# Loading the output weight in 4 KB rows and regrouping the attention outputs with selection matmuls, in a decode-attention kernel

## Chip, cores, metric

One core of one Trainium2 chip. The metric is the device time of one execution in microseconds (us). The span quoted with a profile runs from the first to the last instruction and is mostly about 1.8 us shorter than the time (the changed kernel: 194.7 of 196.47).

## The reference, cut to what matters

```python
B, Sq, D = 32, 1, 512                  # 32 sequences, one new token each
Hq, Hkv, Sk, Dh = 32, 8, 2048, 128
W = 512                                # only the last 512 cached tokens are attended
q = (x @ wq)                           # wq: [512, 4096], bf16
k, v = k_cache[:, :, Sk - W:], v_cache[:, :, Sk - W:]
o = softmax(q k^T * Dh**-0.5) v        # per batch and head
out = o.reshape(B, Sq, Hq * Dh) @ wo   # wo: [4096, 512] bf16, 4 MB
```

All tensors are bf16. The caches' windows are 33.5 MB each, wq and wo 4.2 MB each, so 75.5 MB must come from HBM. The profile of before confirms it: "HBM read 75.53 MB".

## The kernel before, the parts that matter

The core streams K and V of 32 batches through one DMA queue, issued by SyncE (SP). K and V loads are 512 KB each, in rows of 4 KB, one row per partition. TensorE (PE) transposes K, computes scores, transposes the probabilities and multiplies with V (PV). The attention output of a batch, already transposed (`d` on the partitions, 32 heads in the columns), is copied to `oT_sb`. The 4 MB of `wo` are loaded last on the same queue, into the place that `wq` has left, and are contracted with `oT_sb`, head by head.

```python
            sp.wait_ge(pe_qt, 1)
            for c in range(4):                                  # heads 0-9, 10-19, 20-27, 28-31
                h0, h1 = WO_CUT[c], WO_CUT[c + 1]
                sp.dma_start(
                    wo_sb[:, h0:h1, :],
                    wo[h0 * DH:h1 * DH, :].rearrange("(h d) n -> d h n", d=P),   # rows of 1 KB
                ).then_inc(sem_wo[c], 16)
            sp.wait_ge(dve_out, 1)
            sp.dma_start(
                out.rearrange("b s (c n) -> c (b s) n", c=4), out_sb[:, :]       # rows of 256 B
            ).then_inc(sem_out, 16)
# ...
            pe.wait_ge(dve_oT, B)
            for hq in range(HQ):
                if hq in WO_CUT:
                    pe.wait_ge(sem_wo[WO_CUT.index(hq)], 16)
                for c in range(4):                              # four column tiles of PE
                    ins = pe.matmul(
                        KT_ps[:, 0, :].bitcast(F32)[32 * c:32 * (c + 1), 0:128],
                        lhsT=oT_sb[:, :, hq],
                        rhs=wo_sb[:, hq, c * 128:(c + 1) * 128],
                        start=(hq == 0), stop=(hq == HQ - 1), tile_position=(0, 32 * c),
                    )
            ins.then_inc(pe_fin, 1)
# ... VectorE (DVE):
            dve.wait_ge(pe_fin, 1)
            dve.tensor_copy(out_sb[:, :], KT_ps[:, 0, :].bitcast(F32)[:, 0:128]).then_inc(dve_out, 1)
```

Partition `d` must hold row `128 * h + d` of `wo`, because that is where the attention output has its `d`. Consecutive rows of `wo` therefore lie on different partitions, and one contiguous piece is one row of 512 elements: 1 KB.

## Time and profile before

| | before |
|---|---|
| median of 3 runs | 198.06 us (197.87 to 198.22) |
| span of the profiled run | 196.5 us |
| PE / DVE / ACT busy | 73% / 51% / 29% |
| chain that ended last | SP's queue 52%, DMA 37%, PE 7% |

The kernel is bound by its loads. The row of the page that gives the GB/s moved in each of 40 equal slices (4.9 us each) shows it. Only the last four slices fall off.

```profile
GB/s 205 425 417 409 411 405 409 411 409 405 409 409 405 408 407 409 410 407 410 404 409 408 409 409 404 410 406 409 406 408 408 408 409 403 409 404 350 338 253 16
```

The view by windows of the end follows. Its columns are the window, its length, the busy us of each engine with the number of instructions, the granted share of PE's clock, the share of time in which the 16 DMA engines were busy, and the GB/s moved.

```profile
core 0: us, PE busy (x) PEld busy (x) DVE busy (x) ACT busy (x) POOL busy (x), PEclk, DMA share, GB/s
176.00:180.00 4.00, 2.22 (x66) 1.86 (x64) 0.38 (x2) 1.36 (x2) 0.00 (x0) 0.50 1.04 368
180.00:184.00 4.00, 2.02 (x64) 1.87 (x64) 0.38 (x2) 0.00 (x0) 0.00 (x0) 0.50 1.03 343
184.00:189.00 5.00, 1.38 (x44) 1.15 (x48) 0.00 (x0) 0.00 (x0) 0.00 (x0) 0.50 1.04 334
189.00:193.00 4.00, 2.33 (x76) 1.83 (x79) 0.00 (x0) 0.00 (x0) 0.00 (x0) 0.50 0.37 124
```

While `wo` is loaded the DMA engines are as busy as ever (share above 1.0), but move 334 to 368 GB/s instead of 408. After 189 us their share is 0.37 on average. PE's clock stands at half (0.50).

The timeline of the last instructions (start, duration, engine, line, operation, output and inputs, count, and in brackets how long the engine had been idle and what released it):

```profile
191.62 1.08 PE L301 MATMUL KT_ps<-w_sb,oT_sb 128*32 128x128 bf16 x32 [1.41 <-DMA w_sb<-in_wo_dram]
192.95 0.65 PE L301 MATMUL KT_ps<-w_sb,oT_sb 128*32 128x128 bf16 x16 [0.25 <-DMA w_sb<-in_wo_dram]
193.66 0.29 DVE L368 CAST out_sb<-KT_ps 128x128 bf16<-128x128 f32 x1 [10.70 <-PE KT_ps L301]
193.97 0.69 SPq L153 DMA_DIRECT2D out_dram<-out_sb  x1
```

So the end is a chain: the last `wo` load lands at about 192.9, 16 matmuls, one eviction, one store, and the span ends at 196.5.

### The profile page before, as it was taken

Reading aid. Unit: us, or ns where it says so; the run is one execution under the profiler, and the core shown is the slowest. Engines: PE = TensorE matmul, PEld = TensorE weight load, DVE = VectorE, ACT = ScalarE, POOL = GpSimd, SP = SyncE. Lnnn points to the kernel's source line nnn. Section 1 sums busy time; section 2 is a strip of 40 time slices with the busy share of each in tenths; the row PEclk is TensorE's granted clock in tenths of the full one; section 3 lists DMA queues with packets and bytes.
Section 4 is the critical chain, followed back from the end, with each engine's and each line's share of the span. In section 5 each row is a group of like instructions: output and inputs, shape, how many; then the busy total and the mean of one; then the engine's idle time right before and its main releaser. Section 6 shows DMA issues by size and latency. Waiting matters only on the chain.

```text
span 196.5 us, 6073 instructions
## 1 busy us (share of the span) xinstructions
PE 142.8 (73%) x2692; PEld 116.4 (59%) x2692; DVE 99.8 (51%) x187; ACT 56.5 (29%) x67; POOL 12.1 (6%) x43
## 2 busy tenths in 40 slices
PE   0448994987787797749786979779997599746423
PEld 0337773875575576637665858656975477535322
DVE  0006789645774479424952695457645647541000
ACT  3002434433262145203342325232432052320000
POOL 8102000000000010000000000000000000000000
PEclk9999999699999799985999797996699759955555
DMA  5999999999999999999999999999999999999970
GB/s 205 425 417 409 411 405 409 411 409 405 409 409 405 408 407 409 410 407 410 404 409 408 409 409 404 410 406 409 406 408 408 408 409 403 409 404 350 338 253 16
DMA packets 23374, 75.95 MB, mean 386 GB/s; under 512 B 2325, under 2 KB 6453, under 8 KB 22837
## 3 DMA queue, kind: packets, MB, share of 16 engines
q1 hardware_dynamic: 23300, 75.54, 97.5%
q8 instruction: 21, 0.34, 0.7%
q10 hardware_dynamic: 48, 0.03, 0.2%
q14 instruction: 5, 0.03, 0.0%
HBM read 75.53 MB, written 0.03 MB: 384 GB/s over the span
## 4 chain that ended last, share of the span: by engine, by line
SPq 52%; DMA 37%; PE 7%; issue 2%; DVE 0%
DMA K_sb<-in_k_cache_dram 32%; SPq L136 25%; SPq L128 18%; SPq L148 8%; DMA w_sb<-in_wo_dram 5%; PE KT_ps L229 4%; PE QO_ps L279 1%; PE S_ps L246 1%; SPq L122 1%; PE KT_ps L301 0%; SPq L110 0%; DVE out_sb L368 0%
## 5 line engine op out<-in xcount | busy, mean ns | idle before, releaser
L229 PE MATMUL KT_ps<-perm,K_sb 128*128 128x128 bf16 x1024 | 76.0, 238 | 20.7 <-DMA K_sb<-in_k_cache_dram 20.5
L324 DVE COPY KT_sb<-KT_ps 128x1024 bf16<-128x1024 bf16 x96 | 63.3, 687 | 54.0 <-PE KT_ps L229 53.7
L229 PEld LDWEIGHTS KT_ps<-perm,K_sb 128*128 128x128 bf16 x1024 | 67.5, 108 | 27.1 <-DMA K_sb<-in_k_cache_dram 26.0
L383 ACT ACTIVATE KT_sb<-KT_ps 128x1024 bf16<-128x1024 bf16 x32 | 32.7, 1023 | 81.8 <-PE KT_ps L229 81.8
L279 PEld LDWEIGHTS QO_ps<-PT_sb,V_sb 128*128 128x128 bf16 x1024 | 28.2, 98 | 17.4 <-issue 12.7
L279 PE MATMUL QO_ps<-PT_sb,V_sb 128*128 128x16 bf16 x1024 | 31.1, 171 | 3.7 <-DMA V_sb<-in_v_cache_dram 1.9
L346 DVE TENSOR_SCALAR P_ex<-P_f,recip 32x512 bf16<-32x512 f32 x32 | 25.3, 792 | 1.1
L246 PE MATMUL S_ps<-KT_sb,QBD 128*32 128x512 bf16 x256 | 21.4, 414 | 0.0
L401 ACT ACTIVATE PT_sb<-PT_ps 128x1024 bf16<-128x1024 bf16 x16 | 15.5, 1020 | 20.4 <-PE PT_ps L261 20.4
L261 PE MATMUL PT_ps<-ident,P_ex 128*128 128x128 bf16 x128 | 11.8, 266 | 9.6 <-DVE P_ex L346 9.6
L261 PEld LDWEIGHTS PT_ps<-ident,P_ex 128*128 128x128 bf16 x128 | 10.1, 122 | 10.7 <-DVE P_ex L346 10.7
L189 POOL COPY QBD<-QT_sb 128x32 bf16<-128x32 bf16 x32 | 7.4, 245 | 117.9 <-PE S_ps L246 108.0
L353 DVE CAST oT_sb<-QO_ps 128x32 bf16<-128x32 f32 x32 | 5.9, 183 | 8.9 <-PE QO_ps L279 8.8
L301 PE MATMUL KT_ps<-w_sb,oT_sb 128*32 128x128 bf16 x128 | 4.3, 313 | 6.6 <-DMA w_sb<-in_wo_dram 6.6
L207 PE MATMUL PT_ps<-xT_sb,w_sb 128*128 128x32 bf16 x128 | 4.1, 188 | 6.2 <-DMA w_sb<-in_wq_dram 6.2
L301 PEld LDWEIGHTS KT_ps<-w_sb,oT_sb 128*32 128x32 bf16 x128 | 3.3, 158 | 7.4 <-DMA w_sb<-in_wo_dram 4.7
L207 PEld LDWEIGHTS PT_ps<-xT_sb,w_sb 128*128 128x128 bf16 x128 | 3.7, 104 | 6.6 <-DMA w_sb<-in_wq_dram 4.6
L330 DVE TENSOR_REDUCE maxv<-S_ps 128x1 f32<-128x512 f32 x8 | 5.5, 691 | 4.0 <-PE S_ps L246 4.0
L391 ACT ACTIVATE P_f<-S_ps,negmax 128x512 f32<-128x512 f32 x8 | 5.5, 687 | 5.4 <-DVE negmax L332 5.4
L246 PEld LDWEIGHTS S_ps<-KT_sb,QBD 128*32 128x32 bf16 x256 | 3.9, 96 | 3.7 <-issue 1.0
L316 DVE CAST QT_sb<-PT_ps 128x512 bf16<-128x512 f32 x1 | 0.7, 691 | 10.0 <-PE PT_ps L207 10.0
L368 DVE CAST out_sb<-KT_ps 128x128 bf16<-128x128 f32 x1 | 0.3, 292 | 10.7 <-PE KT_ps L301 10.7
(20 smaller groups left out, 11.9 us busy)
## 6 DMA issues: line engine op xcount, KB each, us to landing
K_sb<-in_k_cache_dram SPq DMA_DIRECT2D x64, 512.0 KB, 15.6
V_sb<-in_v_cache_dram SPq DMA_DIRECT2D x64, 512.0 KB, 15.4
w_sb<-in_wq_dram SPq DMA_DIRECT2D x4, 1024.0 KB, 8.4
w_sb<-in_wo_dram SPq DMA_DIRECT2D x2, 1280.0 KB, 19.3
w_sb<-in_wo_dram SPq DMA_DIRECT2D x1, 1024.0 KB, 12.7
w_sb<-in_wo_dram SPq DMA_DIRECT2D x1, 512.0 KB, 9.9
x_sb<-in_x_dram ACTq DMA_DIRECT2D x1, 32.0 KB, 3.2
out_dram<-out_sb SPq DMA_DIRECT2D x1, 32.0 KB
```

The costliest lines, as they stand in the source:

```text
L128: sp.dma_start(K_sb[:, b % NK, h].rearrange("p r d -> p (r d)"), cache_rows(k_cache, b, h)).then_inc(sem_k[b % NK][h], 16)
L136: sp.dma_start(V_sb[:, b % NV, h].rearrange("p r d -> p (r d)"), cache_rows(v_cache, b, h)).then_inc(sem_v[b % NV], 16)
L148: sp.dma_start(wo_sb[:, h0:h1, :], wo[h0 * DH:h1 * DH, :].rearrange("(h d) n -> d h n", d=P),).then_inc(sem_wo[c], 16)
L207: ins = pe.matmul(PT_ps[:, h // 16, :].bitcast(F32)[:, (h % 16) * 32:(h % 16 + 1) * 32], lhsT=wq_sb[:, kt, h * DH:(h + 1) * DH], rhs=xT_sb ...
L229: ins = pe.matmul(KT_ps[:, t, i * 128:(i + 1) * 128], lhsT=K_sb[:, b % NK, h, 8 * (t % 2) + i, :], rhs=perm[:, :, :], start=True, stop=Tru ...
L246: ins = pe.matmul(S_ps[32 * c:32 * c + 32, :], lhsT=QBD[:, b % NQB, g, :], rhs=KT_sb[:, b % NKT, h, :, c, :], start=(j == 0 and h == 0), s ...
L261: ins = pe.matmul(PT_ps[:, r // 8, (r % 8) * 128:(r % 8 + 1) * 128], lhsT=P_ex[:, r, :, :].rearrange("p s g -> p (s g)"), rhs=ident[:, :], ...
L279: ins = pe.matmul(QO_ps[:, 16 * h:16 * h + 16], lhsT=V_sb[:, b % NV, h, r, :], rhs=PT_sb[:, q % 2, r, :].rearrange("p (c n) -> p c n", c=G ...
L324: dve.tensor_copy(KT_sb[:, b % NKT, t // 2, 8 * (t % 2):8 * (t % 2) + 8, :, :], KT_ps[:, t, :]).then_inc(dve_T, 1)
L346: dve.tensor_scalar(P_ex[rows, :, :, c], P_f32[rows, :].rearrange("p (r s) -> p r s", r=NR), recip[rows, q:q + 1], None, op0=ALU.mult,).th ...
L383: act.activation(KT_sb[:, b % NKT, 1, 8:16, :, :], KT_ps[:, 3, :], ACTF.Copy).then_inc(act_T, 1)
L401: act.activation(PT_sb[:, q % 2, 8 * i:8 * i + 8, :].rearrange("p r n -> p (r n)"), PT_ps[:, i, :], ACTF.Copy,).then_inc(act_PT, 1)
```

## The change

The intent: load `wo` in the row size in which K and V move at 403 to 411 GB/s. Partition `m` of chunk `g` now gets the four neighbouring rows `512 * g + 4 * m + i`, one contiguous piece of 4 KB. For that, the attention output must lie the same way: partition `m` must hold `d = (4m + i) mod 128` of head `4g + m // 32`. A 0/1 matrix `band`, made once on GpSimd (POOL), does the regrouping as matmuls: once for batches 0 to 27 (between the PV of batches 28 and 29), once for the last four. The output is stored as 32 rows of 1 KB, for which the four column tiles are evicted into one partition range, two by DVE and two by ScalarE (ACT).

```diff
-    WO_CUT = (0, 10, 20, 28, 32)
+    NHG = HQ // 4
+    SELCUT = 28
-        oT_sb = sb("oT_sb", [P, B, HQ], BF16)
+        oT_sb = sb("oT_sb", [P, HQ, B], BF16)
+        o_sel = sb("o_sel", [P, 4, NHG, B], BF16)
+        band = sb("band", [P, 4, 224], BF16)
-        out_sb = sb("out_sb", [P, 128], BF16)
+        out_sb = sb("out_sb", [32, 4, 128], BF16)
 ... (SP)
-            for c in range(4):
-                h0, h1 = WO_CUT[c], WO_CUT[c + 1]
+            for hg in range(NHG):
                 sp.dma_start(
-                    wo_sb[:, h0:h1, :],
-                    wo[h0 * DH:h1 * DH, :].rearrange("(h d) n -> d h n", d=P),
-                ).then_inc(sem_wo[c], 16)
+                    wo_sb[:, hg].rearrange("p i n -> p (i n)"),
+                    wo[hg * 512:(hg + 1) * 512, :].rearrange("(m i) n -> m (i n)", i=4),
+                ).then_inc(sem_wo[hg], 16)
 ...
-                out.rearrange("b s (c n) -> c (b s) n", c=4), out_sb[:, :]
+                out.rearrange("b s n -> b (s n)"), out_sb[:, :, :].rearrange("b c n -> b (c n)")
 ... (PE)
+            def select(b0, b1, dst):
+                pe.wait_ge(dve_oT, b1)
+                for i in range(4):
+                    for hi in range(4):
+                        ins = pe.matmul(
+                            dst(i),
+                            lhsT=band[:, i, 96 - 32 * hi:224 - 32 * hi],
+                            rhs=oT_sb[:, :, b0:b1].rearrange("p (g hi) b -> p hi g b", hi=4)[:, hi],
+                            start=(hi == 0), stop=(hi == 3), tile_position=(0, 0), skip_group_check=True,
+                        )
+                ins.then_inc(pe_sel, 1)
 ... (after the PV of batch 28)
+                    select(0, nb, ...)
 ... (after the last PV)
+            select(SELCUT, B, ...)
-            for hq in range(HQ): ...
+            for hg in range(NHG):
+                pe.wait_ge(sem_wo[hg], 16)
+                for i in range(4):
+                    for c in range(4):
+                        ins = pe.matmul(
+                            KT_ps[:, 2, :].bitcast(F32)[32 * c:32 * (c + 1), 0:128],
+                            lhsT=o_sel[:, i, hg, :],
+                            rhs=wo_sb[:, hg, i, c * 128:(c + 1) * 128],
+                            start=(hg == 0 and i == 0), stop=(hg == NHG - 1 and i == 3),
+                            tile_position=(0, 32 * c),
+                        )
 ... (DVE)
-                dve.tensor_copy(oT_sb[:, b, :], QO_ps[:, 0:HQ]).then_inc(dve_oT, 1)
+                dve.tensor_copy(oT_sb[:, :, b], QO_ps[:, 0:HQ]).then_inc(dve_oT, 1)
 ... (evictions of the selections, the band on POOL, the output's two copies on DVE and two on ACT: cut)
```

More of the change, by code (lines that the diff above doesn't have):

```diff
@@ L52, in bass_standalone__sliding_block_cached__sampling_kernel @@
         wq_sb = w_sb[:, :].rearrange("p (kt n) -> p kt n", kt=DKT)
-        wo_sb = w_sb[:, :].rearrange("p (h n) -> p h n", h=HQ)
+        wo_sb = w_sb[:, :].rearrange("p (g i n) -> p g i n", g=NHG, i=4)
         K_sb = sb("K_sb", [P, NK, 2, NR, DH], BF16)
@@ L80, in bass_standalone__sliding_block_cached__sampling_kernel @@
         sem_wq = [sem(f"sem_wq{i}") for i in range(DKT)]
-        sem_wo = [sem(f"sem_wo{i}") for i in range(4)]
+        sem_wo = [sem(f"sem_wo{i}") for i in range(NHG)]
         sem_k = [[sem(f"sem_k{i}_{h}") for h in range(2)] for i in range(NK)]
@@ L91, in bass_standalone__sliding_block_cached__sampling_kernel @@
         pe_fin = sem("pe_fin")
+        pe_sel = sem("pe_sel")
+        dve_sel = sem("dve_sel")
+        act_sel = sem("act_sel")
+        act_out = sem("act_out")
+        pool_band = sem("pool_band")
         pool_perm = sem("pool_perm")
@@ L145, in _ @@
             sp.wait_ge(pe_qt, 1)
-            for c in range(4):
-                h0, h1 = WO_CUT[c], WO_CUT[c + 1]
+            for hg in range(NHG):
                 sp.dma_start(
-                    wo_sb[:, h0:h1, :],
-                    wo[h0 * DH:h1 * DH, :].rearrange("(h d) n -> d h n", d=P),
-                ).then_inc(sem_wo[c], 16)
-            sp.wait_ge(dve_out, 1)
+                    wo_sb[:, hg].rearrange("p i n -> p (i n)"),
+                    wo[hg * 512:(hg + 1) * 512, :].rearrange("(m i) n -> m (i n)", i=4),
+                ).then_inc(sem_wo[hg], 16)
+            sp.wait_ge(dve_out, 2)
+            sp.wait_ge(act_out, 2)
             sp.dma_start(
-                out.rearrange("b s (c n) -> c (b s) n", c=4), out_sb[:, :]
+                out.rearrange("b s n -> b (s n)"), out_sb[:, :, :].rearrange("b c n -> b (c n)")
             ).then_inc(sem_out, 16)
@@ L174, in _ @@
             pool.memset(P_ex[:, :, :, :], 0.0).then_inc(pool_ex, 1)
+            pool.memset(band[:, :, :], 0.0).then_inc(pool_band, 1)
+            pool.wait_ge(pool_band, 1)
+            pool.affine_select(
+                out=band[:, :, :], in_=band[:, :, :], compare_op=ALU.not_equal, fill=1.0,
+                base=384, pattern=[[-1, 4], [-4, 224]], channel_multiplier=1,
+            ).then_inc(pool_band, 1)
             pool.wait_ge(pool_init, 4)
@@ L295, in _ @@
                     pt_transposes((it - 5) // 4)
-            pe.wait_ge(dve_oT, B)
-            for hq in range(HQ):
-                if hq in WO_CUT:
-                    pe.wait_ge(sem_wo[WO_CUT.index(hq)], 16)
-                for c in range(4):
-                    ins = pe.matmul(
-                        KT_ps[:, 0, :].bitcast(F32)[32 * c:32 * (c + 1), 0:128],
-                        lhsT=oT_sb[:, :, hq],
-                        rhs=wo_sb[:, hq, c * 128:(c + 1) * 128],
-                        start=(hq == 0), stop=(hq == HQ - 1), tile_position=(0, 32 * c),
-                    )
+                if it == SELCUT + PVLAG:
+                    pe.wait_ge(pool_band, 2)
+                    pe.wait_ge(dve_T, 3 * B)
+                    pe.wait_ge(act_T, B)
+                    nb = SELCUT
+                    select(0, nb, lambda i: KT_ps[:, i // 2, :].bitcast(F32)[
+                        :, (i % 2) * NHG * nb:(i % 2 + 1) * NHG * nb])
+            nl = B - SELCUT
+            select(SELCUT, B, lambda i: KT_ps[:, 3, :].bitcast(F32)[:, i * NHG * nl:(i + 1) * NHG * nl])
+            pe.wait_ge(dve_sel, 2)
+            pe.wait_ge(act_sel, 1)
+            for hg in range(NHG):
[9 more added lines that the diff above has]
+                        )
             ins.then_inc(pe_fin, 1)
@@ L349, in softmax_b, with sel_evac @@
                     ).then_inc(dve_P, 1)
+            def sel_evac(bank, i0, ni, b0, b1):
+                return (
+                    o_sel[:, i0:i0 + ni, :, b0:b1],
+                    KT_ps[:, bank, :].bitcast(F32)[:, 0:ni * NHG * (b1 - b0)].rearrange(
+                        "p (i g b) -> p i g b", i=ni, g=NHG),
+                )
             def ot_evac(b):
                 dve.wait_ge(pe_PV, b + 1)
-                dve.tensor_copy(oT_sb[:, b, :], QO_ps[:, 0:HQ]).then_inc(dve_oT, 1)
+                dve.tensor_copy(oT_sb[:, :, b], QO_ps[:, 0:HQ]).then_inc(dve_oT, 1)
             for it in range(B + PVLAG + 1):
@@ L359, in _ @@
                     ot_evac(it - PVLAG - 1)
+                if it == SELCUT + PVLAG + 1:
+                    dve.wait_ge(pe_sel, 1)
+                    dve.tensor_copy(*sel_evac(0, 0, 2, 0, SELCUT)).then_inc(dve_sel, 1)
                 if it % 4 == 1 and 5 <= it <= B + 1:
@@ L366, in _ @@
                     softmax_a((it - 4) // 4)
+            dve.wait_ge(pe_sel, 2)
+            dve.tensor_copy(*sel_evac(3, 0, 4, SELCUT, B)).then_inc(dve_sel, 1)
             dve.wait_ge(pe_fin, 1)
-            dve.tensor_copy(out_sb[:, :], KT_ps[:, 0, :].bitcast(F32)[:, 0:128]).then_inc(dve_out, 1)
+            for c in range(2):
+                dve.tensor_copy(
+                    out_sb[:, c, :], KT_ps[32 * c:32 * (c + 1), 2, :].bitcast(F32)[:, 0:128]
+                ).then_inc(dve_out, 1)
         @block.scalar
@@ L412, in _ @@
                     pt_evac((it - 5) // 4)
+            act.wait_ge(pe_sel, 1)
+            act.activation(
+                o_sel[:, 2:4, :, 0:SELCUT],
+                KT_ps[:, 1, :].bitcast(F32)[:, 0:2 * NHG * SELCUT].rearrange("p (i g b) -> p i g b", i=2, g=NHG),
+                ACTF.Copy,
+            ).then_inc(act_sel, 1)
+            act.wait_ge(pe_fin, 1)
+            for c in range(2, 4):
+                act.activation(
+                    out_sb[:, c, :], KT_ps[32 * c:32 * (c + 1), 2, :].bitcast(F32)[:, 0:128], ACTF.Copy
+                ).then_inc(act_out, 1)
 _INS = ['x', 'k_cache', 'v_cache', 'wq', 'wo']
```

## The prediction

> **What bounds it now.** The DMA queue. The page's row by slice gives 403 to 412 GB/s from slice 2 to 35. The chain of waits is 52% the queue's own issues plus 37% DMA; PE is 7%. Only the end, from about 176 us, differs. In the windows view 165-176 us moves 408 GB/s, but once the 1 KB rows of wo mix in, 176-180 moves 368, 180-184 343, 184-189 334, all at a DMA share above 1.0: as busy, moving less. From 189 to 193 the share is 0.37: fast engines are done, slow ones lag. The last wo chunk is landed at 192.95, its 16 matmuls take 0.65, the eviction 0.29, the store is issued at 193.97, the span ends at 196.5 (the time is 1.5 above the span).
>
> **What changes.**
> 1. wo comes as 4 KB rows, the form in which K and V already move at 408 GB/s.[...] From 176 us to the end 5.0 MB are moved (sum of 1 us windows). At 408 GB/s the mean engine ends at 188.3 instead of 190.2. The lag from mean engine to landed semaphore is 2.75 us for wo; the same reckoning for the last K load gives 3.3. So I expect the last chunk at about 191.4 (190.9 to 191.9) instead of 192.95: 1.5 us saved. K, with 4 KB rows, has the lag too, so it should stay.
> 2. The first selection (16 matmuls, 224 columns) sits on PE between the PV of batches 28 and 29. At the half clock of this stretch (128 columns took 118 ns) I estimate 187 ns each, 3.0 us. There is no slack: PV of 28 to 31 runs 177.4 to 182.8. PV of 31 then ends near 185.1. Second selection 0.6, its eviction 0.3: wo matmuls start near 186.5, against 185.3 before. 128 of them at 32.5 ns (40 took 1.30 us) take 4.2: PE could end at 190.7, just under the DMA's 191.4 + 0.65. So the selection is nearly hidden, and is the floor if the DMA gains more: about 195.3 us in all.
> 3. The output's eviction becomes two copies in a row on DVE and on ACT, estimated 0.55 us against 0.29 (DVE 128 columns 0.29 each): 0.25 lost.
> 4. The store goes from 128 rows of 256 B to 32 of 1 KB.[...] of the 2.5 us after its issue begins I give 0.1 back.
> 5. Off the path: POOL's band work at the start (about 1.5 us inside 9.9 idle), oT evictions with a 64 B stride (183 ns now), the selections' large evictions (0.7 on DVE and ACT at once, beside PV).
>
> **Sum:** -1.5 +0.25 -0.1 = -1.35: 196.7 us. Range 195.5 to 197.8. Faster by over 2% 0.03, within 2% 0.95, slower 0.02.
>
> **What would show each step.** Windows: 180-188 at 400 GB/s or more. The last wo landing at 191.4 in the chain, which still ends through the wo load, its last 16 matmuls, eviction and store. Timeline: selection 3.0 us after PV of 28, wo matmuls from 186.5, the first chunks found landed, only the last one or two waited for. Out evictions 0.55.
>
> **What would make it wrong.** If the tail's spread of engines comes from the 1 KB rows and shrinks, the PE chain (point 2) becomes the end: 195.3. If the selection or the wo matmuls are slower than estimated, PE ends last and the gain vanishes. If 4 KB rows of wo move no faster than 340, the change costs 0.2 us.

The -0.1 of point 4 was the author's estimate; no trace of before shows it. The 1.5 of point 1 rests on rates measured in before: 408 GB/s with rows of 4 KB, 334 to 368 while the rows of 1 KB load.

## The result

The changed kernel takes 196.45 us (median of 4 runs, 196.38 to 196.48); before, beside it, 198.11. The ratio is 0.9917 with a 95% interval of 0.9900 to 0.9934. Ratios in this document are the mean time of one kernel's fast runs over the mean time of the other's fast runs of the same rounds, so they are not quite the ratio of the medians. Executions over 1.5% slower than the fastest of the same kernel are left out of the means. The output is correct.

The rate by slice, for the changed kernel: the fall to 350 and 338 in slices 36 and 37 is gone.

```profile
GB/s 204 426 420 406 412 405 411 407 410 407 409 407 407 408 408 410 407 407 410 407 407 410 409 407 407 410 406 408 408 406 411 405 410 405 412 405 412 406 251 31
```

The windows of the end, for the changed kernel:

```profile
core 0: us, PE busy (x) PEld busy (x) DVE busy (x) ACT busy (x) POOL busy (x), PEclk, DMA share, GB/s
176.00:180.00 4.00, 2.76 (x45) 2.25 (x43) 0.30 (x1) 1.66 (x2) 0.00 (x0) 0.50 1.03 410
180.00:184.00 4.00, 3.60 (x74) 3.09 (x72) 0.92 (x2) 0.54 (x1) 0.00 (x0) 0.50 1.03 409
184.00:189.00 5.00, 3.85 (x128) 3.49 (x128) 0.88 (x3) 0.00 (x0) 0.00 (x0) 0.50 0.75 299
189.00:193.00 4.00, 1.54 (x53) 0.81 (x48) 0.56 (x2) 0.54 (x2) 0.00 (x0) 0.86 0.15 56
```

Until 184 us `wo` moves at 409 to 410 GB/s. From about 186 on the DMA engines have less and less to move (share 0.95 in 185 to 186, 0.68, 0.57 and 0.50 in the next three us, 0.15 over 189 to 193). In the last window PE's clock is 0.86 instead of 0.50.

The timeline of the end, for the changed kernel, from the first selection (L305) to the store:

```profile
178.59 3.15 PE L305 MATMUL KT_ps<-oT_sb,band 128*128 128x224 bf16 x16
...
185.44 0.30 DVE L397 CAST oT_sb<-QO_ps 128x32 bf16<-128x32 f32 x1 [1.11 <-PE QO_ps L293]
...
185.79 0.61 PE L305 MATMUL KT_ps<-oT_sb,band 128*128 128x32 bf16 x16 [0.39 <-DVE oT_sb L397]
186.44 0.29 DVE L415 CAST o_sel<-KT_ps 128x128 bf16<-128x128 f32 x1 [0.70 <-PE KT_ps L305]
...
186.78 3.00 PE L337 MATMUL KT_ps<-w_sb,o_sel 128*32 128x128 bf16 x96 [0.38 <-DVE o_sel L415]
...
190.41 0.41 PE L337 MATMUL KT_ps<-w_sb,o_sel 128*32 128x128 bf16 x16 [0.63 <-DMA w_sb<-in_wo_dram]
...
191.66 0.41 PE L337 MATMUL KT_ps<-w_sb,o_sel 128*32 128x128 bf16 x16 [0.83 <-DMA w_sb<-in_wo_dram]
192.12 0.56 ACT L473 ACTIVATE out_sb<-KT_ps 32x128 bf16<-32x128 f32 x2 [9.80 <-PE KT_ps L337]
192.12 0.59 DVE L418 CAST out_sb<-KT_ps 32x128 bf16<-32x128 f32 x2 [5.39 <-PE KT_ps L337]
192.77 0.36 SPq L161 DMA_DIRECT2D out_dram<-out_sb  x1
```

PE starts on `wo` at 186.78 and does the first six chunks without a wait; for the last two it waits for the DMA. So the loads still end last, and the selection lies in front of loads that have not landed yet.

The difference of the two profiled spans, 1.85 us, can be laid out along this chain (all from the two timelines and spans; the store ends with the span):

| piece of the end | before | after | difference |
|---|---|---|---|
| last 16 matmuls start (last load landed) | 192.95 | 191.66 | -1.29 |
| from there to the eviction | 0.71 | 0.46 | -0.25 |
| eviction to the store's issue | 0.31 | 0.65 | +0.34 |
| store's issue to the end of the span | 2.56 | 1.91 | -0.65 |

### The profile page after: what moved, and what is told of

It reads as the page before. It is cut to its first block, busy times and chain, and to the rows that moved or that the text cites. A ratio compares the mean times of both kernels' runs of the same rounds, so it can differ in the third digit from the quotient of the medians.

```text
span 194.7 us, 6153 instructions
## 1 busy us (share of the span) xinstructions
PE 144.0 (74%) x2724; PEld 114.9 (59%) x2724; DVE 102.1 (52%) x190; ACT 57.6 (30%) x70; POOL 15.0 (8%) x45
## 4 chain that ended last, share of the span: by engine, by line
SPq 68%; DMA 23%; PE 5%; issue 3%; DVEq 0%; DVE 0%
SPq L144 37%; SPq L136 26%; DMA K_sb<-in_k_cache_dram 15%; DMA w_sb<-in_wo_dram 8%; SPq L155 5%; PE KT_ps L243 4%; SPq L130 1%; PE S_ps L260 1%; PE QO_ps L293 0%; PE KT_ps L337 0%; SPq L118 0%; DVEq L47 0%; DVE out_sb L418 0%
## 5 line engine op out<-in xcount | busy, mean ns | idle before, releaser
L243 PE MATMUL KT_ps<-perm,K_sb 128*128 128x128 bf16 x1024 | 75.2, 235 | 22.4 <-DMA K_sb<-in_k_cache_dram 22.2
L243 PEld LDWEIGHTS KT_ps<-perm,K_sb 128*128 128x128 bf16 x1024 | 65.6, 106 | 30.0 <-DMA K_sb<-in_k_cache_dram 28.4
L260 PE MATMUL S_ps<-KT_sb,QBD 128*32 128x512 bf16 x256 | 22.2, 428 | 0.0
L203 POOL COPY QBD<-QT_sb 128x32 bf16<-128x32 bf16 x32 | 8.5, 279 | 116.1 <-PE S_ps L260 108.1
L275 PE MATMUL PT_ps<-ident,P_ex 128*128 128x128 bf16 x128 | 9.4, 231 | 9.8 <-DVE P_ex L383 9.8
L275 PEld LDWEIGHTS PT_ps<-ident,P_ex 128*128 128x128 bf16 x128 | 7.9, 104 | 10.9 <-DVE P_ex L383 10.8
L397 DVE CAST oT_sb<-QO_ps 128x32 bf16<-128x32 f32 x32 | 9.3, 289 | 7.5 <-PE QO_ps L293 7.5
L337 PE MATMUL KT_ps<-w_sb,o_sel 128*32 128x128 bf16 x128 | 3.8, 289 | 1.9 <-DMA w_sb<-in_wo_dram 1.5
L337 PEld LDWEIGHTS KT_ps<-w_sb,o_sel 128*32 128x32 bf16 x128 | 2.9, 131 | 2.7 <-DMA w_sb<-in_wo_dram 2.2
L427 ACT ACTIVATE QT_sb<-PT_ps 128x512 bf16<-128x512 f32 x1 | 0.6, 597 | 12.0 <-PE PT_ps L221 12.0
```

The costliest lines, as they stand in the source:

```text
L243: ins = pe.matmul(KT_ps[:, t, i * 128:(i + 1) * 128], lhsT=K_sb[:, b % NK, h, 8 * (t % 2) + i, :], rhs=perm[:, :, :], start=True, stop=Tru ...
L260: ins = pe.matmul(S_ps[32 * c:32 * c + 32, :], lhsT=QBD[:, b % NQB, g, :], rhs=KT_sb[:, b % NKT, h, :, c, :], start=(j == 0 and h == 0), s ...
L275: ins = pe.matmul(PT_ps[:, r // 8, (r % 8) * 128:(r % 8 + 1) * 128], lhsT=P_ex[:, r, :, :].rearrange("p s g -> p (s g)"), rhs=ident[:, :], ...
L397: dve.tensor_copy(oT_sb[:, :, b], QO_ps[:, 0:HQ]).then_inc(dve_oT, 1)
```

## The experiments

Twelve kernels were run in three calls of four, a1 to a4, b1 to b4 and c1 to c4, each call on another chip; the kernel before ran beside each call (median 198.06, 198.40 and 198.09). A landing time below comes from one profiled execution. Five profiles with 4 KB rows and much the same program on PE (the changed kernel, a2, a3, c3, c4) have the last landing at 191.61, 191.29, 191.07, 191.45 and 191.24, so differences of landings below about 0.5 us mean little. Some give a wrong result, as said there. Two views are used that are not lines of the page: the trace keeps the time of every increment of a load's semaphore, 16 for each load of 512 KB, as many as the page counts DMA engines; and it keeps the start and the length of every DMA packet, those of the instruction queue (q8) among them. An increment is called a landing here. That each one comes from an engine of its own is the author's reading and not shown: neither increments nor packets name an engine. The prediction and the expectations speak of fast and slow engines in this sense. Numbers from these are in plain fences.

### 1. Row size alone: a1_rows_1k and b1_rows_1k_b

```diff
 (changed kernel)
-                    wo_sb[:, hg].rearrange("p i n -> p (i n)"),
-                    wo[hg * 512:(hg + 1) * 512, :].rearrange("(m i) n -> m (i n)", i=4),
+                    wo_sb[:, hg],
+                    wo[hg * 512:(hg + 1) * 512, :].rearrange("(i m) n -> m i n", i=4),
```

The result is wrong: the rows lie in another order than the selection expects. Expected:

> The changed kernel with one thing undone: each of the 8 wo loads of 512 KB comes in 1 KB rows again (wrong result on purpose, the rows lie in another order than the selection expects). Theory A (the gain at the end is the row size): 180 to 188 us moves about 340 GB/s again, the last wo chunk lands near 193.0 instead of 191.6, time 197.6 to 198.0. Rival B (the gain is the division into 8 equal chunks): the landing stays at 191.6 and the time at 196.4.

> The kernel of a1_rows_1k once more (wrong result on purpose), because its profiled execution fell in a slow state of 377 us. Theory A: about 340 GB/s from 180 to 188 us, last wo landing near 192.7 to 193.0, time 197.4 to 197.7.

The three fast runs of a1 took 197.45 to 197.66 us, ratio 0.9977 (0.9960 to 0.9994) to before, where the changed kernel has 0.9917. Its profiled execution was one of 377 us, in which PE was the limit throughout (the transposing matmul at a mean of 478 ns instead of 235); it is not used, and its cause is open. The second submission ran once, in 197.86 us beside 198.40 (0.9973 by these two numbers; a single run, so its state is unknown), and gave a usable profile. Its windows:

```profile
180.00:184.00 4.00, 3.22 (x82) 2.82 (x81) 1.22 (x3) 0.54 (x1) 0.00 (x0) 0.84 1.03 327
184.00:189.00 5.00, 3.52 (x124) 3.05 (x120) 0.59 (x2) 0.00 (x0) 0.00 (x0) 0.57 1.05 347
```

and its last matmuls of the `wo` product:

```profile
192.71 0.62 PE L337 MATMUL KT_ps<-w_sb,o_sel 128*32 128x128 bf16 x16 [0.69 <-DMA w_sb<-in_wo_dram]
```

327 and 347 GB/s at full DMA share: eight equal chunks in 1 KB rows are as slow as four unequal ones. The last load landed at 192.67. Theory A holds: the row size is what moved the landing. It is worth about 1.2 us (0.9977 against 0.9917, 0.6% of 198; the two intervals make that 0.7 to 1.7 us), of which about 0.2 goes with PE's clock, since in this run the last 16 matmuls took 0.62 us at half clock.

### 2. The output end alone: c1_store_only

```diff
 (kernel before)
-        out_sb = sb("out_sb", [P, 128], BF16)
+        out_sb = sb("out_sb", [32, 4, 128], BF16)
-                out.rearrange("b s (c n) -> c (b s) n", c=4), out_sb[:, :]
+                out.rearrange("b s n -> b (s n)"), out_sb[:, :, :].rearrange("b c n -> b (c n)")
-            dve.tensor_copy(out_sb[:, :], KT_ps[:, 0, :].bitcast(F32)[:, 0:128]).then_inc(dve_out, 1)
+            (two copies of 32 partitions on DVE, two on ACT, as in the changed kernel)
```

> The kernel before with only the output end of the change: evictions as two copies each on DVE and ACT, store as 32 rows. Theory A (the end's part of the gain, apart from the loads): store 1.95 us from its issue to the end instead of 2.55, evictions 0.59 instead of 0.29, so 0.3 faster than before: ratio about 0.9985. The wo loads unchanged: last landing about 192.9. Rival B (most of the 1.6 us came from the end): ratio under 0.994.

Measured: ratio 0.9983 (0.9971 to 0.9995), as theory A had it. The end of its timeline:

```profile
193.39 0.59 DVE L371 CAST out_sb<-KT_ps 32x128 bf16<-32x128 f32 x2 [10.71 <-PE KT_ps L303]
193.39 0.57 ACT L420 ACTIVATE out_sb<-KT_ps 32x128 bf16<-32x128 f32 x2 [16.13 <-PE KT_ps L303]
194.05 0.36 SPq L155 DMA_DIRECT2D out_dram<-out_sb  x1
```

The span ends at 196.0, so the store takes 1.9 us from its issue; before it took 2.56. The copies, two in a row instead of one, cost 0.3. The last `wo` landing was at 192.64, not apart from the 192.91 before. Rows (1.2 us) and output end (0.34 us, 0.17% of 198, by the interval 0.1 to 0.6) together give about 1.5 of the 1.65 us; what is left is smaller than the intervals.

### 3. Why the store is faster: a2_store_256

```diff
 (changed kernel)
-        out_sb = sb("out_sb", [32, 4, 128], BF16)
+        out_sb = sb("out_sb", [32, 4, 160], BF16)       # padded, so that pieces are 256 B
-                out.rearrange("b s n -> b (s n)"), out_sb[:, :, :].rearrange("b c n -> b (c n)")
+                out.rearrange("b s (c n) -> b (s c) n", c=4), out_sb[:, :, 0:128]
```

> The changed kernel with the output stored as 128 rows of 256 B (padded tile), but with 32 partitions outermost instead of 4 blocks. The store took 1.93 us from issue to the end of the span in the changed kernel and 2.57 before. Theory A (before was slow because its outermost dimension of 4 left the store on 4 of the 16 DMA engines, which the 5 semaphore records of that store in the trace suggest): 16 engines here, so 1.9 to 2.1, time within 0.2 us of 196.45. Rival B (rows of 256 B are slow in themselves): 2.5 again, time 197.0.

Measured: 196.66 us, ratio 0.9929, correct. The time is 0.21 above 196.45, at the edge of the 0.2 us that theory A allowed, but the store itself is not what A said:

```profile
192.46 0.68 SPq L161 DMA_DIRECT2D out_dram<-out_sb  x1
```

The span ended at 194.9, so the store took 2.4 us, nearer to rival B's 2.5 than to A's 1.9 to 2.1. This run's loads had landed 0.3 us earlier than in the other profile, which hides it in the profiled time. From the packets of the three stores:

```
store of                       landings  issue to first packet  packets  last packet to landing
before (4 x 32 rows of 256 B)      4            1.30             0.52            0.34
a2     (128 rows of 256 B)        16            1.32             0.32            0.34
after  (32 rows of 1 KB)          16            0.86             0.29            0.36
```

The store before has an outermost dimension of 4 and only 5 semaphore records, one at 195.05, before its first packet, and four landings at 196.08 to 196.13; the other two have 16. But having four landings instead of 16 goes with only 0.2 us (0.52 against 0.32, both in rows of 256 B). The larger part, 0.45, passes before the first packet, with the issue that lasts 0.69 us before, 0.68 in a2 and 0.36 after. Both slow issues cut the output and the tile differently on the two sides; the fast one is 32 equal rows on both. They also have 128 rows instead of 32, and no run separated the two. The shortest issues of the loads speak for the cut: `wq` and the 4 KB `wo` loads, 128 equal rows on both sides, issued in 0.41 to 0.44 us, K loads, also 128 rows but cut into 32 by 4 on the HBM side, in about 0.6. That is a comparison, not a test. To move, 256 B rows were hardly slower here (0.32 against 0.29), so rival B's reason is not what the packets show.

### 4. Is the selection hidden: a3_no_select

```diff
 (changed kernel: both calls of select, their waits and their evictions taken out)
+            pe.wait_ge(dve_oT, B)
-                            lhsT=o_sel[:, i, hg, :],
+                            lhsT=oT_sb[:, 4 * hg + i, :],
```

Its output is wrong, which doesn't matter for the time.

> The changed kernel without both selections and their evictions; the last matmuls read the attention outputs directly (wrong result on purpose). Theory A (selection is hidden behind the wo load): the last wo chunk still lands near 191.6, the time stays within 0.3 us of 196.45, perhaps 0.2 above it, since PE would be idle before the last chunk and its 16 matmuls take 0.65 us at the half clock instead of 0.41. Rival B (selection is on the path): PE's work ends earlier and the time falls by 1 us or more.

Measured: 196.20 us, ratio 0.9908 (0.9893 to 0.9923), within 0.3 us of the changed kernel and not apart from it. The last chunk's matmuls:

```profile
191.12 0.61 PE L327 MATMUL KT_ps<-w_sb,oT_sb 128*32 128x128 bf16 x16 [0.62 <-DMA w_sb<-in_wo_dram]
```

PE now waits before every chunk but the first and stays at half clock (0.50 from 176 to 193), so its last 16 matmuls take 0.61 instead of 0.41 us. Selection is hidden. What gave PE more than its half clock at the end of the changed kernel is not shown: c3 below does nearly the same work on PE as a2 until 188.9 us, and 16 of its matmuls took 0.62 us at 188.96, as long as in a3 at half clock, where a2's took 0.41 at 188.85 (clock 0.88 from 189 to 193).

### 5. Where the rest of the load's gain went

The loads should have gained more. The 16 landings of the last `wo` load (us from the start of the span):

```
before: mean 190.81   189.3 189.3 189.4 189.5 189.9 189.9 190.0 190.2 190.8 191.0 191.3
                      192.2 192.3 192.3 192.6 192.9                              mean to last 2.10
after:  mean 188.71   186.09 186.42 186.44 186.56 186.68 187.16 187.23 | 188.40
                      189.15 189.53 189.96 | 190.96 191.02 191.03 191.08 191.61   mean to last 2.90
```

The mean landing gained 2.1 us, the last one, which PE waits for, 1.3. (In c4, the changed kernel again: mean 188.75, last 191.24, mean to last 2.48.) In the changed kernel the 16 landings come in groups, spread over 5.5 us. What goes with the late ones? The pages have a line for the instruction queue (packets, MB, share of 16 engines), first of the kernel before, then of the changed one:

```profile
q8 instruction: 21, 0.34, 0.7%
q8 instruction: 22, 0.36, 0.8%
```

22 packets of 16 KB, one about every 8.6 us, each 1.0 to 1.2 us long. The page counts 2,724 matmuls and as many loads of weights on PE, and its trace has 150 semaphore instructions there: 5,598 instructions, 254 for each packet. The number of packets follows PE's instructions in the runs below: 2,040 more on PE in b2 gave 30 packets, 1,920 fewer in b4 gave 14. No view names such a packet as what PE waited for. The theory tested here, A in the expectations, was that these packets go with the late landings; in what way one could delay a load is not shown by any trace. The packets' lengths come back after eight, in b4 and c2 as well (here the changed kernel's, ns; only the 1st does not fit); what that means is open:

```
packets  1 to  8: 1036 1084 1069 1105 1108 1095 1033 1032
packets  9 to 16: 1087 1079 1065 1105 1106 1095 1021 1031
packets 17 to 21: 1082 1079 1075 1108 1098
```

21 of them started before the last landing.

**a4_k8_2** loaded the last two chunks with an outermost dimension of 8; the last chunk then had eight landings instead of 16.

```diff
 (changed kernel, last two chunks)
+                    bass.AP(tensor=wo.tensor, offset=hg * 512 * D, ap=[[4 * D, 8], [32 * D, 16], [1, 4 * D]])
-                    wo[hg * 512:(hg + 1) * 512, :].rearrange("(m i) n -> m (i n)", i=4),
```

> The changed kernel with the last two wo chunks loaded by an access pattern whose outermost dimension is 8, so that only 8 of the 16 DMA engines move them (rows land in another order, wrong result on purpose). In the changed kernel the 16 engines finish the last chunk from 186.1 to 191.6[...]. Theory A[...]: if the 8 used are the fast ones, the last landing falls to about 189.7 and the time to about 194.8; if they are the slow ones, it rises to about 194.1 and the time to about 199. Rival B (which engines lag has nothing to do with a fixed half): slow engines are in both halves, the last landing rises by 1 to 2.5 us.

The result is wrong (the rows are permuted). Measured: 201.71 us, ratio 1.0184, last landing 196.95: neither A nor B in size. Of the changed kernel's 16 landings seven came by 187.23 and nine from 188.40 on (not eight and eight; b3's "fast eight" are these seven). Here the eight of the last chunk spread from 192.1 to 196.95, about as wide as the changed kernel's 16 (5.5 us), so no set of early or of late ones alone is seen. The mean of the eight landings moved by 3.27 us from one chunk to the next; with 64 KB for each (512 KB by eight), that is an estimated 20 GB/s each, against 25.5 before (408 / 16), so the spread is not clean evidence. Whether the number of landings or the permuted rows did that was not separated. The trick does not work, and it says nothing for or against the packets.

**b2_pe_fill**, **b3_pool_fill** and **c2_mm_fill** added instructions without effect.

```diff
 b2: +                if 1 <= it <= 30:
     +                    for _ in range(136): pe.wait_ge(pe_xT, 1)       # built as 68 instructions
 b3: +                if 1 <= b <= 30:
     +                    for _ in range(136): pool.wait_ge(pool_init, 4)
 c2: +                if 1 <= it <= 30:
     +                    for _ in range(34):
     +                        pe.matmul(QO_ps[:, 256:260], lhsT=ident[:, :], rhs=ident[:, 0:4], ...)
```

> The changed kernel plus 2040 instructions without effect on PE (waits that are already met, 68 in each of 30 iterations, none in the last ones). The changed kernel shows 22 packets of 16 KB on the instruction queue, about one per 8.6 us, of 1.0 to 1.1 us each, and the spread of the 16 landings of a K load grows by about 1.2 us at every eighth of them. Theory A[...]: 30 packets, 27 or 28 of them before the last wo landing[...], so the last wo landing moves from 191.5 to 192.4 to 193.0, the time to 197.3 to 198.0[...]. Rival B (the lag of engines has other reasons): more packets, but the last landing stays within 0.4 of 191.5 as long as PE keeps pace. If PE itself becomes slower than the loads, the DMA share falls below 1.0 before 185 us and the run tells nothing.

> The same 2040 instructions on POOL, which is idle for nine tenths of the time, so that PE's instruction stream and pace stay as they are. Theory A: again 8 packets more; last wo landing 192.4 to 193.0[...], or unchanged at 191.5 but with the fast eight later[...]. Rival B: all landings as in the changed kernel.

> The changed kernel plus 1020 small matmuls without effect (4 columns, 34 in each of 30 iterations, none in the last)[...]. Theory A[...]: 30 packets of instructions instead of 22[...], so the last wo landing moves by one step of about 1.4 us, to about 193.0[...], the time rises by about 1.4. Rival B (fewer PV matmuls helped in some other way): the landings stay as in the changed kernel. If PE falls behind the loads, the DMA share before 180 us falls below 1.0 and the run tells nothing.

All three slowed the engine that carried them below the pace of the loads: 408.85, 224.92 and 210.49 us. By the condition set beforehand for b2 and c2, their times and their last landings tell nothing (c2's rate falls to 369 and 343 GB/s in slices 32 and 33, after 168 us, and its last `wo` load lands 18 us before the span ends). b3's packets did not even go where expected: q8 stayed at 22 and another queue, q14, grew from 4 to 20 of 8 KB, so the 22 go with PE's instructions. (The step of about 1.4 us in c2's expectation was the author's estimate, from the distance between b4's groups of landings, below.)

But c2 kept full rate until 168 us, and there it is the best test of all, because it moves the times of the packets and leaves the loads as they are. (Its profiled run counts as slow, 210.9 us of span against 207.6 of its fastest; what follows compares none of its run times, only at which packet its spread jumps, before 135 us.) The spread is the last minus the first of the 16 landings of one K load:

```
                     1st packet   spread       9th packet   spread       17th packet  spread
changed kernel         15.1    0.94 -> 2.10      85.5    2.46 -> 3.59      153.8    4.07 -> 5.03
c2 (more on PE)        14.7    0.63 -> 1.51      68.5    2.17 -> 3.06      122.0    3.75 -> 4.62
b4 (fewer on PE)       15.2    1.09 -> 2.02     115.0    2.42 -> 3.19      (only 14 packets)
```

The second number is that of the first K load to land fully after the packet (by 17, 88 and 159 us in the changed kernel). The jump of about 1 us comes with the 1st, 9th and 17th packet, wherever these fall in time; around 85 us, where the changed kernel jumps, c2 stays at 3.7 and b4 at 2.65. There are smaller ones, of 0.6 to 0.7, at the 2nd, 10th and 18th in the changed kernel and in c2, and of 0.7 to 0.8 at the 3rd and the 11th in b4; between them the spread stays within 0.3. So the jumps move with the packets. A cause in time or in the bytes moved would have left them where they were. Why they return after eight packets is not shown.

**b4_pv_1** took instructions away: one PV matmul instead of 16 per batch and half of the heads. The result is wrong; all data loads are unchanged.

```diff
-                    for r in range(NR):
+                    for r in range(1):
-                            start=(r == 0), stop=(r == NR - 1), tile_position=(0, 0),
+                            start=True, stop=True, tile_position=(0, 0),
```

> The changed kernel with only 1 of the 16 PV matmuls per batch and group of heads (wrong result on purpose): 960 matmuls and their loads of weights fewer on PE, all DMA traffic of data unchanged. Theory A: 14 packets of instructions instead of 22[...], so the last wo landing falls from 191.5 to about 189.3, and the time to 194.2 to 194.7. Rival B (the lag has other reasons, or the loads are bound by bytes alone): last landing within 0.4 of 191.5, time 196.2 to 196.6.

Measured: 195.66 us beside 198.40, ratio 0.9865 (0.9845 to 0.9886), against 0.9917 of the changed kernel: about 1.0 us faster, half of what theory A had said, and not the nothing of rival B. The instruction line of its page:

```profile
q8 instruction: 14, 0.23, 0.5%
```

14 packets, as expected. The landings of the last chunk:

```
b4: 186.58 186.68 186.90 187.06 187.10 187.34 187.45 | 188.34 188.43 188.52 188.79
    | 189.73 189.74 189.79 190.15 190.47          mean 188.32, mean to last 2.15
```

The earliest seven landings are where they were (186.6 to 187.5, in the changed kernel 186.1 to 187.2), the last is 1.1 us earlier, at 190.47 instead of 191.61. The 189.3 that had been expected was the author's estimate, with 1.2 us for a packet, about the first jump of the K loads' spread (0.94 to 2.10). The landings form groups of seven, four and five, near 187.0, 188.5 and 190.0, 1.5 us apart. Against c4's 191.24 the last is 0.8 earlier. The time agrees: 1.1 from the landing, less 0.2 because its last 16 matmuls ran at half clock (0.62 us), is the 0.9 between the two spans. PE is also far less busy in b4, so the run alone would not settle the cause; together with the moved jumps of c2 it ties the late landings to the packets that follow PE's instructions. How these act on a load is not shown.

Why the kernel before, with 21 packets as well, had less lag at its end (2.10) can be read from b1, which differs from the changed kernel in the row size alone. The spread of the 16 landings, from the first `wo` load to the last, and the last load's landings:

```
                     spread            first landing   last landing   mean to last
before (1 KB)      5.29 -> 3.60           189.31          192.91          2.10
b1     (1 KB)      5.19 -> 3.48           189.19          192.67          1.92
after  (4 KB)      5.64 -> 5.52           186.09          191.61          2.90
```

So the shorter lag goes with the rows of 1 KB: in b1 the first landing comes 3.1 us later than in the changed kernel, the last 1.1 us later. Why the first one moves more is open. In before the DMA share dips to 0.92 and 0.91 at 180 and 184 us; b1 shows the same shrinking with a share of 1.03 and 1.05 over 180 to 184 and 184 to 189 us, so the dips are not needed for it.

### 6. A smaller last load: c3_split_last, with c4_after beside it

```diff
 (changed kernel: the last wo load as two loads of 2 KB rows, each with its own semaphore)
+                    for e in range(2):
+                        sp.dma_start(wo_sb[:, hg, 2 * e:2 * e + 2], rows[:, 2 * e:2 * e + 2]).then_inc(sem_wo[hg + e], 16)
 ... (PE, before i == 2 of the last chunk)
+                        pe.wait_ge(sem_wo[NHG], 16)
```

> The changed kernel with the last wo load cut into two halves in 2 KB rows, so that only 8 matmuls instead of 16 wait for the last landing. If the row of 2 KB costs little, 0.1 to 0.2 us faster than the changed kernel of the same call; if 2 KB rows cost as 1 KB rows do, 0.1 slower.

> The changed kernel again, beside the other runs of this call: ratio 0.990 to 0.9935, last wo landing 191.2 to 191.7.

c4 gave 0.9920 (0.9907 to 0.9934), median 196.36, last landing 191.24: the result holds on another occasion. c3 gave 0.9910 (0.9897 to 0.9923), median 196.26. The direction is the expected one, but 0.1 us is inside the intervals. The profile could not show the gain either:

```profile
191.49 0.41 PE L345 MATMUL KT_ps<-w_sb,o_sel 128*32 128x128 bf16 x8 [0.23 <-DMA w_sb<-in_wo_dram]
```

The last 8 matmuls took 0.41 us, as long as 16 at full clock in the changed kernel (clock 1.00 from 191 to 192). No correct version was found that is clearly better than the changed kernel.

## Why the prediction was right, point by point

The prediction said 196.7 us (195.5 to 197.8), within 2% with 0.95; measured 196.45. Its sum was -1.35 us; the times moved by 1.65.

1. **The loads, -1.5: right in the cause and, within the spread between profiles, in size.** Row size is the cause (a1 and b1: slower by about 1.2 us and 327 to 347 GB/s when it is undone). The last load was in use at 191.66 instead of the predicted 191.4, so 1.29 us were gained; in c4 it was 191.28. The mean landing gained 2.1 us (1.9 predicted), and the lag from mean to last took 0.8 back (0.4 in c4). The prediction kept the lag because K loads have it too, and feared that it might come from the 1 KB rows and shrink. Keeping it was right, and b1 shows the opposite of the fear: with 1 KB rows the lag is shorter. Why K loads have it was not known then; in the runs it grows in jumps with the packets of PE's instructions (0.94 us of spread before the 1st, 5.03 after the 17th). One of the signs to look for was stated wrongly: "180-188 at 400 GB/s or more". The rate held to 185 (414 in 184 to 185, then 381 and 274 in the next two us), as the last load's first landings come from 186.1 on. A mean end at 188.3, in the same text, already implied that.
2. **The selection, hidden: right.** 3.15 us (3.0 predicted; its 187 ns for each matmul is less than the 206 that 118 ns for 128 columns gives in proportion, and 197 were measured), second one 0.61 (0.6), its eviction 0.29 (0.3), `wo` matmuls from 186.78 (186.5) at 31 ns each (32.5), only the last two chunks waited for. Taking selection out altogether gained no more than noise (a3). Missed: PE had more than its half clock at the end (0.86 in the last window), so the last 16 matmuls took 0.41 us instead of 0.65. What gave it back was not tested, and it does not always come (c3). This term of -0.25 was absent from the sum.
3. **The evictions, +0.25: right.** 0.59 us for the two copies on each engine (0.55 predicted).
4. **The store, -0.1: the term that was mis-sized.** It measured -0.65 in the profiles and, in the times of c1 with the evictions' +0.3 in it, -0.34. The prediction reasoned from the size of a row (256 B and 1 KB rows on 16 landings moved in 0.32 and 0.29 us). The packets show 0.45 in the time before the first packet and 0.2 in moving them, with four landings before and sixteen after. The trace of before already held a sign of the second part: 5 semaphore records for this store, 16 for each load.
5. **Off the path: right, with one difference.** The evictions of `oT_sb`, which now write with a stride of 64 bytes, take 289 ns instead of 183. Four of them lie in the PV chain of the last batches, and the selection's slack absorbs it. Why the stride costs 106 ns was not tested. The band work on POOL took 1.8 us (about 1.5 predicted), the selections' large evictions 0.62 us on DVE and 0.54 on ACT (0.7 predicted).

The errors had opposite signs in part (the loads gained 0.2 less, store and clock together 0.8 more than thought), so it is partly luck that the total came within 0.3 us.

## What to carry to other kernels

In a load-bound kernel ask for the last landing, not for the mean rate: the loads' mean landing here gained 2.1 us and the last landing 1.3 of them, because PE waits for the last of a load's 16 landings (191.61; its matmuls start at 191.66). In this kernel the length of PE's program goes with that tail: with 14 packets of instructions instead of 22, and a less busy PE (b4), the last landing came 0.8 to 1.1 us earlier. And look at a small final store as closely as at a big load: it sits whole on the end of the chain (2.56 us here before, 1.91 after), and its issue time and its number of landings can be read off the trace.
